# A new order of all steps, with one weight cast cut in two and one PSUM value cut in two, in a explicitly scheduled kernel of gated attention and MLP

## The chip, the cores and the metric

The kernel runs on one core of one Trainium2 chip. The metric is the device time of one execution in microseconds; the kernel before has a median of 178.71 us over three runs (177.62 to 179.46).

## The reference

Two parts follow one another. The first is a recurrence with a gate per element; its result, reshaped to 3072 tokens of 384 values, is the input of an MLP whose activation is h times cos h.

```python
B, H, S, D = 4, 8, 768, 48
f = 1.0 / (1.0 + np.exp(-f_logit))
state = np.zeros((B, H, D, D))
for t in range(S):
    state = f[:, :, t, :, None] * state + np.einsum('bhd,bhe->bhde', k[:, :, t], v[:, :, t])
    y[:, :, t] = np.einsum('bhd,bhde->bhe', q[:, :, t], state)
x = y.transpose(0, 2, 1, 3).reshape(3072, 384)
h = x @ w_in                  # 384 x 2048
out = (h * np.cos(h)) @ w_out # 2048 x 384
```

## The kernel before

**Tiles.** The recurrence is done in chunks of 128 tokens. A *pair* n is two chunks of one batch, 256 tokens with all 8 heads; there are 12 pairs, three to a batch, and the state starts anew with every third. Inside a chunk the gates are summed as logarithms (on TensorE, step `cum`), and q and k are multiplied by the exponentials of that sum and of its negative, so that the chunk becomes ordinary matmuls: scores of k and q, masked, times v, plus q times the state. The MLP takes the 256 tokens of one pair as one *unit* m: eight h steps (step h m.j s: quarter j of the 2048 columns, half s, six matmuls each), four cosines and four products, then for each of its two tiles of 128 tokens four output steps (step o, four matmuls each).

**Engines and steps.** The steps of pair n and unit m, with the lines that they come from:

- loads `f`, `k`, `q`, `v` (L334) and of the weights `w` (L318; `w0.i` is quarter i of w_in, `w1.i` quarter i of w_out), nearly all on SP's queue. Pairs 0 and 1 are loaded by halves (`f0.0`, `f0.1`).
- the weights' casts to bf16, `wc` (L195). A weight quarter is loaded into a buffer that otherwise holds the products g; the buffer is free again when the cast has read it.
- the gate on ACT (ScalarE): `ex`, `ln` (L370, L376), `fx`, `fy` (L387, L390), and after `cum` the exponentials `eb`, `ei` (L470, L474, L479). On POOL (GpSimd) `ad` (L408) sums parts of the logarithms, `ka` and `qa` (L394, L384) multiply by f, `km` and `qm` (L501, L505) make the scaled k and q, called qk.
- q and k transposed: in pairs 0 to 3 by TensorE (`tq`, `tk`, L573) with a copy out of PSUM (`qkt`, L195); in pairs 4 to 11 by DMA transposes from SP's queue (`tq`, L556).
- v spread over the rows that the matmuls want: in pairs 0 and 1 `vb` (L516), then `vs` on TensorE (L529) and two copies `vt`; in the others copies alone.
- TensorE: scores `sc` (L593), state `ps` (L614, L624), outputs `y` and `yi` (L678). DVE (VectorE): the mask `am` (L597), the state's sums and decay `st`, `sz` (L645, L650); `sj` is on TensorE. `xe` (L195) copies y out of PSUM as the MLP's x.
- MLP: `h` (L726) on TensorE, the cosine `co` (L731) on ACT, the product `g` (L708) on DVE, `o` (L747) on TensorE, the copy `ot` (L195) and the store `out` (L758).
- `zf` (L300): matmuls of zeros on TensorE before there is data. `cq`, `z`, `ctl`: constants.

ACT has two tables of functions, one for Exp and Ln and one for Sin; each change of the one for the other is a table load (L790), 12 in the program.

**Order.** `describe` only declares the steps with what they read and write. A string `ORDER` sets the order: one word a step, with its engine (T TensorE, S ScalarE, V VectorE, G GpSimd, Y SyncE) and the numbers of the buffers or PSUM banks that it writes to. `emit` issues the steps in that order; each engine runs its own in that order and waits where an input is missing or a buffer is not yet free. PSUM has eight banks: a value of pool `p1` is one bank, one of `p2` two neighbours, such as every h value (1024 columns) and every score. `apart` tells the framework that steps in different banks of one PSUM tile don't depend on each other. So `co1.2:S1` reads: the second-last cosine of unit 1, on ACT, into buffer 1.

**Course.** PE begins with zeros and the halves of pairs 0 and 1; unit 0's first full h run, step `h0.10`, comes at 24.9 us. Units 0 and 1 are worked together, then 2 and 3, and so on, with the recurrence of later pairs between them. Their h steps come as runs, with cosines and products following: between two such runs ACT does the gates of the next two pairs, with the other table loaded.

## Time and profile before

| | |
|---|---|
| median of three runs | 178.71 us (177.62, 178.71, 179.46) |
| the profiled execution | 179.52 us |
| its span, first to last instruction | 177.7 us |
| TensorE busy, share of the span | 170.9 us, 96% |
| VectorE, ScalarE, GpSimd busy | 74%, 73%, 55% |
| granted TensorE clock over the span | 1.00 |
| DMA | 34.46 MB, mean 194 GB/s |
| last matmul's end to the span's end | 3.0 us |

The device time of the profiled execution is 1.8 us longer than its span. TensorE is the busiest engine by far, but a busy share says little of a single place: between two runs of h steps TensorE works on outputs of the units before, while ACT changes its table, does the gates and changes it back. In a row of a timeline the columns are the start (us), the duration, the engine, the line, the operation with tile names without buffer numbers, and in brackets the idle time before it with what ended it. Rows of a table of windows give the window, its length and then, for PE, PEld (weight loads), DVE, ACT and POOL in this order, the busy time with the number of instructions; last come the granted clock, the share of the DMA engines and GB/s.

### The profile page before, as it was taken

What the parts mean: (1) busy time and instruction counts of PE and PEld (TensorE: products, weight loads), DVE (VectorE), ACT (ScalarE), POOL (GpSimd) and SP (SyncE); (2) the same over time, 40 slices, a digit from 0 to 9 for tenths busy, and PEclk for the clock granted to TensorE, in tenths of its full rate; (3) what the DMA queues carried; (4) which work ended last, traced back from release to release, by engine and by line L of the source; (5) the groups of instructions that cost most, each with busy time, mean ns of one, the idle gap of its engine ahead of it and who ended that gap; (6) DMA issues with size and microseconds to landing.
All of it is one profiled execution on the core that took longest, in us unless ns stands there. A gap on an engine that the chain in (4) does not pass through costs nothing.

```text
span 177.7 us, 5995 instructions
## 1 busy us (share of the span) xinstructions
PE 170.9 (96%) x2565; PEld 126.4 (71%) x2568; DVE 131.9 (74%) x208; ACT 130.0 (73%) x177; POOL 98.3 (55%) x125
## 2 busy tenths in 40 slices
PE   7999999999999999999969999999999999999993
PEld 2576678866778767787647886676786767887762
DVE  6378989786696899799957688878878967274720
ACT  3977698659999999769978789988693644374610
POOL 7042397796579989989737977369993000000000
PEclk9999999999999999999999999999999999999999
DMA  4999999999998999987999999982077040001033
GB/s 128 302 308 355 267 353 315 337 301 311 254 269 204 205 221 227 267 210 133 199 221 284 279 185 268 218 229 76 4 162 162 4 177 4 4 0 44 4 133 133
DMA packets 70330, 34.46 MB, mean 194 GB/s; under 512 B 59296, under 2 KB 68768, under 8 KB 70304
## 3 DMA queue, kind: packets, MB, share of 16 engines
q1 hardware_dynamic: 69744, 33.69, 78.5%
q10 hardware_dynamic: 560, 0.39, 0.8%
q8 instruction: 20, 0.33, 0.8%
q14 instruction: 6, 0.05, 0.2%
HBM read 25.17 MB, written 4.72 MB: 168 GB/s over the span
## 4 chain that ended last, share of the span: by engine, by line
PE 57%; DMA 16%; POOL 10%; SPq 10%; ACT 2%; issue 2%; DVE 1%; POOLq 0%; DVEq 0%
PE ps L747 28%; PE ps L726 21%; SPq L334 8%; DMA k<-in_k_dram 7%; POOL qk L505 6%; DMA q<-in_q_dram 5%; DMA qkt<-qk 4%; PE ps L678 4%; PE ps L593 3%; ACT co L731 1%; SPq L318 1%; POOL q L384 1%; POOL k L394 1%; PE ps L624 1%; POOL vt L195 1%
## 5 line engine op out<-in xcount | busy, mean ns | idle before, releaser
L708 DVE TENSOR_TENSOR g<-ps,co 128x1024 bf16<-128x1024 f32 x48 | 57.9, 1222 | 19.6 <-ACT co L731 18.3
L747 PE MATMUL ps<-w_out_bf,g 128*128 128x384 bf16 (+1 forms) x400 | 68.5, 320 | 0.0
L731 ACT ACTIVATE co<-ps,halfpi 128x1024 bf16<-128x1024 f32 x48 | 52.7, 1113 | 21.1 <-PE ps L726 19.9
L726 PE MATMUL ps<-x,w_in_bf 128*128 128x256 bf16 x576 | 67.4, 273 | 0.0
L726 PEld LDWEIGHTS <-w_in_bf 128*128 128x128 bf16 x576 | 55.4, 98 | 8.5
L747 PEld LDWEIGHTS <-g 128*128 128x128 bf16 x400 | 37.2, 98 | 20.7
L597 DVE TENSOR_TENSOR am<-ps,pmask 128x1024 bf16<-128x1024 f32 x24 | 28.9, 1220 | 6.1 <-PE ps L593 5.8
L790 ACT ACT_TABLE_LOAD x12 | 15.4, 1283 | 1.7 <-PEq L855 1.5
L505 POOL TENSOR_TENSOR qk<-k,bi 128x384 bf16<-128x384 f32 x16 | 16.0, 1000 | 0.5
L505 POOL TENSOR_TENSOR qk<-q,b 128x384 bf16<-128x384 f32 x16 | 15.9, 999 | 0.6
L195 POOL COPY vt<-vb 64x384 bf16<-64x384 bf16 x27 | 13.5, 501 | 1.3
L195 ACT COPY ot<-ps 128x384 f32<-128x384 f32 (+1 forms) x13 | 5.5, 441 | 9.6 <-PE ps L747 9.1
L408 POOL TENSOR_TENSOR sp<-ls 128x384 bf16<-128x384 f32 x8 | 8.0, 998 | 7.9 <-ACT ls L376 7.7
L370 ACT ACTIVATE f<-f 128x768 f32<-128x768 f32 (+1 forms) x14 | 10.2, 746 | 1.3 <-DMA f<-in_f_logit_dram 1.3
L300 PE MATMUL ps<-zero 128*128 128x512 bf16 x31 | 9.6, 434 | 1.6 <-DVE zero L201 1.2
L645 DVE TENSOR_TENSOR ps<-ps,sz 128x192 f32<-128x192 f32 x26 | 9.4, 363 | 1.7 <-PE ps L624 0.9
L593 PE MATMUL ps<-qkt 48*64 48x128 bf16 x384 | 9.1, 220 | 1.5 <-DMA qkt<-qk 1.4
L394 POOL TENSOR_TENSOR k<-k,f 128x384 f32<-128x384 f32 x8 | 8.0, 1002 | 4.4 <-ACT bi L479 2.5
L593 PEld LDWEIGHTS <-qkt 48*64 48x64 bf16 x384 | 6.2, 106 | 5.2 <-issue 2.5
L195 DVE COPY ot<-ps 128x384 f32<-128x384 f32 (+1 forms) x13 | 6.9, 535 | 3.6 <-PE ps L747 3.6
L195 DVE CAST x<-ps 128x384 bf16<-128x384 f32 x14 | 7.3, 552 | 2.7 <-PE ps L678 2.7
L384 POOL TENSOR_TENSOR q<-f,q 128x384 f32<-128x384 f32 x8 | 8.0, 999 | 1.7 <-ACT f L387 1.5
(105 smaller groups left out, 185.9 us busy)
## 6 DMA issues: line engine op xcount, KB each, us to landing
out_dram<-ot SPq DMA_DIRECT2D x22, 192.0 KB, 2.8
f<-in_f_logit_dram SPq DMA_DIRECT2D x10, 384.0 KB, 5.6
k<-in_k_dram SPq DMA_DIRECT2D x10, 384.0 KB, 5.7
q<-in_q_dram SPq DMA_DIRECT2D x10, 384.0 KB, 5.5
v<-in_v_dram SPq DMA_DIRECT2D x10, 384.0 KB, 5.4
g<-in_moe_w_in_dram SPq DMA_DIRECT2D x4, 768.0 KB, 7.2
g<-in_moe_w_out_dram SPq DMA_DIRECT2D x4, 768.0 KB, 8.5
q<-in_q_dram SPq DMA_DIRECT2D x4, 192.0 KB, 4.6
```

What stands on the lines that cost most here:

```text
L195: (nc.scalar.copy if e == "ACT" else eng(e).tensor_copy)(out=o, in_=i)
L334: G.step(name, ("SP", "ACT") if name in ("f0.0", "f0.1") else ("SP",), lambda e: eng(e).dma_start(out=val.ap.rearrange("p (r f) e d -> p r ...
L370: nc.scalar.activation(out=flat(t.ap), in_=flat(t.ap), func=AF.Exp, scale=-1.0)
L384: eng(e).tensor_mul(out=w.ap[:, :, 0, :], in0=t.ap[:, :, 1, :], in1=w.ap[:, :, 0, :])
L505: G.step(f"{nm}{n}.{u}", ("POOL", "DVE") if cut else ("POOL",), lambda e, u=u, j=j, src=src, dec=dec: eng(e).tensor_mul(out=qkp[u][j].ap[: ...
L593: nc.tensor.matmul(o[64 * h:64 * h + 64, r, 2 * a + g, :].rearrange("p (e n) -> p e n", e=2), lhsT=qkv(u)[s, 1, a, g, h, :], rhs=qkv(u)[s, ...
L597: G.step(f"am{n}.{u}", ("DVE",), lambda e, u=u, sc=sc: nc.vector.tensor_mul(out=am[u].ap.rearrange("p r b n -> p (r b) n"), in0=sc.ap.rear ...
L708: nc.vector.tensor_mul(out=o.rearrange("p b (n e) -> p b n e", e=2), in0=ph.ap.rearrange("p (b e n) -> p b n e", e=2, n=64), in1=co.ap.rea ...
L726: nc.tensor.matmul(ph.ap[:, i * T:(i + 1) * T].rearrange("p (g t) -> p g t", t=C), lhsT=w_in_bf[:, kk, f0:f0 + 128], rhs=xa[:, :, kk, :], ...
L731: G.step(f"co{m}.{j}", ("ACT",), lambda e, ph=ph, co=co: nc.scalar.activation(out=co.ap, in_=ph.ap, func=AF.Sin, bias=halfpi), reads=[ph], ...
L747: nc.tensor.matmul(po.ap[:, 0:w], lhsT=gT.ap[:, j, i * C:(i + 1) * C], rhs=w_out_bf[:, j, a * w:a * w + w], start=(po.first and j == 4 * s ...
L790: nc.scalar.preload_act_table_set(TABLES[s.table])
```

## The change

Four things change in the code; the other lines are as before (those behind the insertions stand 2 to 10 lines lower, so L556 becomes L565 and L790 becomes L800).

1. `ORDER` is replaced as a whole: order, engines, buffers and banks. Steps on SP 103 to 102 (`f0.1` goes to ACT's queue), on ACT 169 to 177, on VectorE 188 to 186, on GpSimd 113 to 109. GpSimd gives up `km0.1`, `km3.0` and `km3.1` (to VectorE) and `wc1.3` (to ACT). The two-tile value of the last tile but one, tile 22, was cut in two already and stays so.
2. `ZEROS` goes from 34 to 30.
3. The cast `wc0.0` of the first quarter of w_in is two steps, one for each half of the columns: `wc0.00`, now on ACT, and `wc0.01`, on GpSimd. An h step that needs one half waits for that alone.
4. In pairs 0 and 1 the spread v is two values of one PSUM bank each instead of one of two banks. One step `vs` still writes both; each copy `vt` reads one.

```diff
-ZEROS = 34
+CUT_W = ((0, 0),)
+ZEROS = 30
...
 ORDER = """
...
-w1.3:Y4 tk2.1:T3 tq2.1:T h1.31:T4 h1.30:T co0.2:S0 tq2.0:T2 g0.2:V tk2.0:T co1.3:S2 wc1.0:G h1.21:T6
...
-qm7.1:G tq7.1:Y1 q8:Y2 h5.11:T vt6.0:G o7.2:T0 qa6:G co5.1:S1 qm6.1:G tq6.1:Y3 o7.3:T vt6.3:S g4.1:V
...
+wc0.3:G h0.20:T0 g1.1:V0 co1.0:S1 h0.21:T qm2.1:G tk2.1:T3 g1.0:V co0.2:S2 h1.31:T4 f4:Y2 qm2.0:G
...
+co4.1:S1 tq7.1:Y3 h5.21:T qm6.1:G st6.10:V vb7:S0 o6.0:T g4.1:V tq6.1:Y1 vt6.0:G0 co5.2:S3 h5.11:T2
...
         G.step(f"w{part}.{i}", ("SP",), fetch, writes=[stage])
-        G.step(f"wc{part}.{i}", ("POOL", "ACT"), lambda e: copy(e, dst.ap, view()),
-               reads=[stage], writes=[dst])
+        if (part, i) not in CUT_W:
+            G.step(f"wc{part}.{i}", ("POOL", "ACT"), lambda e: copy(e, dst.ap, view()),
+                   reads=[stage], writes=[dst])
+            return
+        for a in range(2):
+            cols = lambda t, a=a: t[:, :, a * w // 2:(a + 1) * w // 2]
+            to = dst.part(cols)
+            G.step(f"wc{part}.{i}{a}", ("POOL", "ACT"), lambda e, to=to, cols=cols: copy(e, to.ap, cols(view())),
+                   reads=[stage], writes=[to])
...
-            pv = Val(p2)
+            pv = [Val(p1), Val(p1)]
...
-                                rows = pv.ap.rearrange("p (g x) -> p g x", g=2)[64 * x:64 * x + 64, g, 0:DM]
+                                rows = pv[g].ap[64 * x:64 * x + 64, 0:DM]
...
-                    pv.ap[:, 512 * g:512 * g + DM].rearrange("p (h d) -> p h d", d=D)), reads=[pv], writes=[vtp[g]])
+                    pv[g].ap[:, 0:DM].rearrange("p (h d) -> p h d", d=D)), reads=[pv[g]], writes=[vtp[g]])
...
-                G.step(f"h{m}.{j}{s}", ("PE",), first, reads=[xw, w_in_v[(j * F + s * F // 2) // 4]],
+                wv = w_in_v[(j * F + s * F // 2) // 4]
+                G.step(f"h{m}.{j}{s}", ("PE",), first, reads=[xw, wv.parts[s] if wv.parts and F == 4 else wv],
```

In `ORDER` the new string differs everywhere. Three places bear on the prediction.

**ScalarE from the table load behind unit 1's cosines to the gate of pair 5.** Names: `ps_...` is a PSUM tile, `g_...` the staging buffer of a weight. Before, `f_101` is the gate of pair 4 and `f_99` that of pair 5, `qkt_139` the copy `qkt3.0`, the cast is `wc1.2`:

```order
L195 COPY qkt_139<-ps_170 128x1024
L790 ACT_TABLE_LOAD
L370 ACTIVATE f_101<-f_101 128x768
L376 ACTIVATE ls_115<-f_101 128x768
L390 ACTIVATE f_101<-ls_115 128x8x48
L195 COPY vt_136<-vb_128 64x8x48
L387 ACTIVATE f_101<-f_101 128x8x48
L195 CAST w_out_bf<-g_156 128x1536
L195 COPY vt_136<-vb_128 64x8x48 x2
L195 COPY vt_134<-vb_126 64x8x48
L195 COPY ot_164<-ps_171 128x384
L370 ACTIVATE f_99<-f_99 128x768
```

The same stretch after; here `qkt_137` is `qkt3.0`, `g_158` holds `w1.3` and `g_156` `w1.2`:

```order
L800 ACT_TABLE_LOAD
L379 ACTIVATE f_101<-f_101 128x768
L197 COPY qkt_137<-ps_172 128x1024
L385 ACTIVATE ls_115<-f_101 128x768
L197 CAST w_out_bf<-g_158 128x1536
L396 ACTIVATE f_101<-f_101 128x8x48
L197 COPY vt_136<-vb_128 64x8x48 x2
L197 CAST w_out_bf<-g_156 128x1536
L399 ACTIVATE f_101<-ls_115 128x8x48
L197 COPY vt_136<-vb_128 64x8x48
L197 COPY ot_166<-ps_171 128x384
L197 COPY vt_134<-vb_127 64x8x48
```

The table load now stands ahead of `qkt3.0`, which has moved behind the first Exp of pair 4, and a second cast, `wc1.3`, stands in the stretch; behind the Exp and Ln of pair 5 follows an x copy, `xe2.0`, that VectorE did before.

**SyncE at the load of pair 4's gate.** `f_101` is `f4`, `g_158` is `w1.3`, `k_105` (before) and `k_104` (after) are `k3`. Before:

```order
L334 DMA k_105<-in_k_dram 128x8x96
L318 DMA g_158<-in_moe_w_out_dram 128x4x384
L334 DMA f_101<-in_f_logit_dram 128x8x96
L334 DMA v_109<-in_v_dram 128x8x96
L318 DMA g_156<-in_moe_w_out_dram 128x4x384
```

After, the same five loads:

```order
L343 DMA k_104<-in_k_dram 128x8x96
L343 DMA f_101<-in_f_logit_dram 128x8x96
L320 DMA g_158<-in_moe_w_out_dram 128x4x384
L343 DMA v_109<-in_v_dram 128x8x96
L320 DMA g_156<-in_moe_w_out_dram 128x4x384
```

The load of `f4` and that of `w1.3` have changed places.

**SyncE at the transposes of pairs 7 and 6.** `qk_125` is the scaled q and k of pair 7, `qk_124` that of pair 6; `q_108` is `q8` before. Before:

```order
L334 DMA f_99<-in_f_logit_dram 128x8x96
L334 DMA f_101<-in_f_logit_dram 128x8x96
L556 DMA_TRANSPOSE qkt_139<-qk_125 128x8x128
L556 DMA_TRANSPOSE qkt_138<-qk_125 128x8x128
L334 DMA q_108<-in_q_dram 128x8x96
L556 DMA_TRANSPOSE qkt_140<-qk_124 128x8x128
L758 DMA out_dram<-ot_166 128x384
L758 DMA out_dram<-ot_163 128x384
L556 DMA_TRANSPOSE qkt_137<-qk_124 128x8x128
L334 DMA q_107<-in_q_dram 128x8x96
```

And after:

```order
L343 DMA f_101<-in_f_logit_dram 128x8x96
L343 DMA f_102<-in_f_logit_dram 128x8x96
L565 DMA_TRANSPOSE qkt_139<-qk_125 128x8x128
L565 DMA_TRANSPOSE qkt_140<-qk_125 128x8x128
L565 DMA_TRANSPOSE qkt_138<-qk_124 128x8x128
L565 DMA_TRANSPOSE qkt_137<-qk_124 128x8x128
L768 DMA out_dram<-ot_164 128x384
L343 DMA q_107<-in_q_dram 128x8x96
```

The load of `q8` no longer stands between the transposes, and the two stores that stood ahead of the last of them are gone from there.

Two smaller places that the prediction uses: at the start, SyncE's last load of the halves is `v1.1` where it was `k1.1`; and behind `vs1`, TensorE's order has `sj1.0` before the state of pair 1. The score steps of pair 3, `sc3.0` and `sc3.1`, stood side by side and now have output steps and `sc3.1` ahead of `sc3.0` between them.

## The prediction

> **What bounds the kernel now.** I read the page's busy shares first, then a table of windows, then the chain of waits, then the timelines of the engines at the few places where TensorE (PE) stands still.

> ```profile
> PE 170.9 (96%) x2565; PEld 126.4 (71%) x2568; DVE 131.9 (74%) x208; ACT 130.0 (73%) x177; POOL 98.3 (55%) x125
> 24.90:174.70 149.80, 148.06 (x2151) 111.43 (x2144) 113.83 (x157) 111.59 (x145) 87.77 (x103) 1.00 0.79 181
> ```

> The second row is a window: its length, then each engine's busy time. From 24.9 us, where the first full tile of the MLP begins (step h0.10), until the last matmul, PE is idle for 149.80 - 148.06 = 1.74 us, at full clock (1.00). From h0.10 on both orders hold the same 270 PE steps. So behind that point the change can only win what PE waits, lose new waits, or move the point itself; behind the last matmul the same copies and stores follow in both, 3.0 us to the span's end at 177.7.

> The waits, from PE's own timeline and the chain:

> ```profile
> 30.84 0.40 PE L573 MATMUL ps<-ident,qk 128*128 128x128 bf16 x4 [0.24 <-POOL qk L501]
> 85.23 4.07 PE L747 MATMUL ps<-w_out_bf,g 128*128 128x384 bf16 x24
> 90.75 0.64 PE L593 MATMUL ps<-qkt 48*64 48x128 bf16 x32 [1.45 <-DMA qkt<-qk]
> 82.75 1.02 POOL qk L505 x2
> 83.77 6.95 DMA qkt<-qk
> 79.37 3.15 SPq L556 DMA_TRANSPOSE qkt<-qk  x2
> 82.58 0.57 SPq L334 DMA_DIRECT2D q<-in_q_dram  x1
> 83.77 1.24 SPq L556 DMA_TRANSPOSE qkt<-qk  x1
> DMA to landing us min/median/max: 3.0/3.5/6.9
> ```

> One wait is large. At 90.75 the scores sc6.1 begin 1.45 us late: their transposed operand (tq6.1) left SP at 83.77, when POOL's last product for it was done, and took 6.95 us, the longest of 16 (median 3.5, last row). A load of q (q8, 82.58) stood ahead of it.

> The second thing to see is a stretch where PE never waits and yet is paced by others:

> ```profile
> 39.27 1.01 ACT L195 COPY qkt<-ps 128x1024 bf16<-128x1024 bf16 x1 [1.93 <-PE ps L573]
> 40.30 1.28 ACT L790 ACT_TABLE_LOAD   x1
> 41.59 0.84 ACT L370 ACTIVATE f<-f 128x768 f32<-128x768 f32 x1
> 44.60 1.46 ACT L195 CAST w_out_bf<-g 128x1536 bf16<-128x1536 f32 x1
> 47.92 0.84 ACT L370 ACTIVATE f<-f 128x768 f32<-128x768 f32 x1
> 50.57 0.49 ACT L479 ACTIVATE bi<-ps 128x384 f32<-128x384 f32 x1
> 52.41 1.28 ACT L790 ACT_TABLE_LOAD   x1
> 53.71 4.18 ACT L731 ACTIVATE co<-ps,halfpi 128x1024 bf16<-128x1024 f32 x4
> 54.85 4.62 DVE L708 TENSOR_TENSOR g<-ps,co 128x1024 bf16<-128x1024 f32 x4 [1.40 <-ACT co L731]
> 41.60:53.70 12.10, 12.10 (x238) 8.56 (x237) 9.90 (x20) 11.84 (x19) 8.49 (x11) 1.00 1.14 276
> ```

> From 41.59 to 53.7 ACT (ScalarE) is busy 11.84 of 12.10 us, without a pause worth naming; the cosines can start only at 53.71, behind the second table load. The products g follow on DVE, 4.62 us for four, so the second ends near 54.85 + 2 x 1.16 = 57.2. Four PSUM pairs of banks hold the first products h of this run; a later one takes the pair that the second g frees (h2.01 here), so it can't begin before 57.2, and PE, without an idle moment there, arrives just then. ACT's second table load sets that moment as much as PE does.

> **The change part by part.** The sum is made against the profiled execution (179.52 us, span 177.7), which lies 0.81 above the median of the runs, 178.71; I carry the difference over to the median.

> The start. Before h0.10, PE waits for loads. The one that lands last ahead of the weights:

> ```profile
> 12.02 5.83 DMA k<-in_k_dram
> 17.39 0.94 ACT L516 ACTIVATE vq<-v,odd 128x768 bf16<-128x768 f32 x1
> 19.70 0.52 PE L529 MATMUL ps<-vq,qsel 64*64 64x192 bf16 x16
> 21.82 0.82 PE L726 MATMUL ps<-x,w_in_bf 128*128 128x256 bf16 x6
> L195 POOL CAST w_in_bf<-g 128x1536 bf16<-128x1536 f32 x4 | 5.9, 1465 | 5.5 <-DMA g<-in_moe_w_in_dram 5.5
> L300 PE MATMUL ps<-zero 128*128 128x512 bf16 x31 | 9.6, 434 | 1.6 <-DVE zero L201 1.2 <-issue 0.3
> ```

> It is k1.1, at 17.85; now v1.1 is last, behind the same bytes, so at about 17.85 too. Then vb1.0 on ACT (0.94) gives 18.85, and PE has vs1 and everything up to h0.10 before it. In this trace PE needs 24.90 - 19.70 = 5.2 us from vs1 to h0.10; sj1.0, which now stands behind vs1, adds 0.26 and a wait of sc1.1 for DVE's copy perhaps 0.2: 18.85 + 5.2 + 0.45 = 24.5, a gain of 0.4, between 0.9 (neither counts) and a loss of 1.0 (v1.1 landing 1.4 later). The halved cast of w_in costs POOL 0.73 instead of 1.465 and ACT about 0.8 (half of its 1.46 for a whole w_out cast, 0.73, is the low end); PE reaches h0.00 after both, so it is hidden by PE's own work; uncovered it would cost the 0.8. The two single-bank values for spread v cost nothing: same matmuls, same copies. Four zero matmuls fewer are 4 x 0.215 = 0.9 us of filler before data (9.6 us for 31, the first ones slow); PE would otherwise wait there, so I count nothing, and 0.9 if they were in the way.

> None of this is a term yet, because the ACT stretch takes it back. With the wait at 30.84 gone too (the q-transpose now comes three h steps later), PE would stand 1.0 us ahead at 57. What ACT allows is less. Its new order moves the table load ahead of qkt3.0, whose 1.93 us of waiting it fills: behind the cosine of h0.31 the load starts at about 36.2 instead of 40.30. Then three more pieces of work stand in the stretch: the qkt3.0 copy (1.01), a second w_out cast, wc1.3 (1.46), and an x copy, xe2.0 (0.48). The first Exp needs f4, which SP now issues right behind k3, ahead of w1.3:

> ```profile
> 29.45 0.50 SPq L334 DMA_DIRECT2D k<-in_k_dram  x1
> DMA to landing us min/median/max: 7.4/7.4/7.4
> 20.00:40.00 20.00, 19.71 (x312) 15.88 (x302) 17.25 (x21) 13.84 (x14) 16.59 (x14) 1.00 1.09 316
> ```

> k3 landed at 36.9. The DMA engines were full (share 1.09) at 316 GB/s, at which the 384 KB of f4 take 1.25 us and the 768 KB of w1.3 2.5. So I put f4's landing at 38.4, and at 40.4 or more where it stood before. From there, each step as long from start to start as the trace has its kind (large activations 0.88, small ones 0.43): 38.4 + 0.88 (ex4) + 1.01 + 0.87 (ln4) + 1.46 + 0.43 + 0.92 (two vt) = 43.97, then wc1.2 1.48, fx4 and vt2.1 0.93, ot3 and vt3.2 0.85 = 47.23. The Exp of f5 can't start before f5 lands:

> ```profile
> 39.53 1.32 SPq L334 DMA_DIRECT2D f<-in_f_logit_dram  x1
> DMA to landing us min/median/max: 7.8/7.8/7.8
> ```

> That is 39.53 + 7.8 = 47.35; before it started at 47.92. From it to the table load are 52.41 - 47.92 = 4.49 us, plus 0.43 for xe2.0, less 0.15 for a short wait on PE: the load at 47.35 + 4.77 = 52.12 and the cosines 0.3 earlier than now. So the term is **-0.3**; ACT reaches f5 with 0.1 us to spare. The low end is -1.0 (f5 lands 0.7 earlier, PE's whole lead kept), the high end +1.6 (f4 lands 2 us later, as before the swap).

> The transposes. POOL's work from ad5 to the last product for tq6.1 is one 0.5 us copy less, and ad5 starts with ln5's end, about 0.6 earlier. Here it ran 49.79 to 83.75, of which 1.3 were waits:

> ```profile
> 49.79 0.99 POOL L408 TENSOR_TENSOR sp<-ls 128x384 bf16<-128x384 f32 x1 [1.86 <-ACT ls L376]
> 65.40 1.00 POOL L408 TENSOR_TENSOR sp<-ls 128x384 bf16<-128x384 f32 x1 [0.50 <-ACT ls L376]
> 76.32 1.00 POOL L394 TENSOR_TENSOR k<-k,f 128x384 f32<-128x384 f32 x1 [0.67 <-ACT co L731]
> ```

> So the product is ready at 49.2 + 33.96 - 0.5 = 82.6, or 81.3 without those waits, and q8 no longer stands between the transposes. With 3.1 us to land (the two at 79.37 were 2 us apart, so they don't hold each other up) that is 85.7; with 6.95 it is 89.6. sc6.1 now comes at about 88.5 in PE's order. I take **-1.45** (nearer to the median landing of 3.5); the far end leaves 1.1 of the wait.

> PE's tilings. The order splits sc3.0 from sc3.1, so behind h0.10 stand 22 stretches of small-tile matmuls instead of 21. What a stretch costs beside full-size steps:

> ```profile
> 94.60 0.76 PE ps L747 x4
> 95.36 0.65 PE ps L726 x6
> 159.69 0.65 PE ps L747 x4
> ```

> An output step of four matmuls takes 0.65 among its like and 0.76 next to such a stretch, 0.11 at each edge: **+0.2** for one stretch, 0 to 0.5. [...]

> Sum: -0.3 - 1.45 + 0.2 = -1.55, so 177.97 for the execution profiled and 178.71 - 1.55 = **177.2** for the median. One per cent, 1.79 us here, is about what a measurement of this kernel can tell from no change.

> **The rivals.**
> A, the larger gain: f5 lands earlier and ACT doesn't hold PE back. For it: from 18 to 47 us SP waited for staging buffers of the weights (row below), which are now handed out in another order, so loads may be issued sooner. Against it: the DMA engines were full (1.09 and 1.14 in the window rows), so fewer waits of SP bring no bytes. Then -1.0 - 1.45 = -2.45, 176.3.

> ```profile
> SPq L318 <- POOL w_in_bf L195: 5.1, 2, 3.6
> ```

> B, the wait was this execution's own. For it: the fastest run is 177.62, 1.9 under the profiled one, and a transpose of 6.95 stands alone. Against it: the median is nearer to the profiled one. Then a typical run gains only the 0.3, less 0.2 for the stretch, 178.6.

> C, slower: ACT's stretch becomes the new bound. Its place is between the two table loads. For it: 2.9 us of work more and only 0.1 to spare before f5, and the first Exp now waits for f4 with qkt3.0 and wc1.3 behind it. Against it: the table is there four us earlier. Each us that f4 lands after 38.5 delays the cosines, and PE with them, by one: with f4 1.65 us later than I put it, the gain is gone. Behind the 2.5 us of bytes of w1.3 and the 1.25 of one load more it lands 3.75 later, 3.65 past what ACT has to spare: -0.3 + 3.65 - 1.45 + 0.2 = +2.1, 180.8.

> **How the numbers follow.** Forecast 0.42, A 0.26, B 0.14, C 0.18. The forecast's own range is 176.2 to 178.0, and 0.16 of its 0.42 lies under 176.9; with A that is 0.42 for faster by over 1%. Of C I put 0.10 over 180.5. The rest, 0.48, is within 1%. Range 175.8 to 179.3: A with the run-to-run spread at the low end, half of C at the high end.

> **What would show it.** Right: no wait of sc6.1 and sc7.1 over 0.3 us near 88; two table loads near 36 and 52, ACT filled between; the first cosine behind the second at 53.4; span near 176.2. Wrong: first cosine after 55 (C); h0.10 after 25.5, or waits of PE over 0.5 us at places that I don't name (before sc9.0, or where cum6 waits for POOL); a first cosine before 52.9 (A).

## The result, and the profile after

The change makes the kernel slower. Its median is 180.47 us (179.71 to 181.75, six runs) against 178.63 us for the kernel before (six runs): the ratio is 1.0122, with a 95% interval of 1.0085 to 1.0158. That is 1.84 us more, where 1.5 us less was forecast, and above the range.

The profiled execution of the change took 179.71 us, the shortest of its six, and that of the kernel before 179.52 us, above its six others. So these two traces lie closer together (spans 177.9 and 177.7) than the medians. Later I took five more traces of the change and one more of the kernel before (`before_again`, span 176.7, an execution of 178.52 us), and the reading below is over all of them.

The busy shares have hardly moved, except that ScalarE does more and GpSimd less:

```profile
PE 171.3 (96%) x2562; PEld 126.1 (71%) x2564; DVE 131.2 (74%) x206; ACT 135.4 (76%) x184; POOL 92.4 (52%) x121
```

The table of windows, from the first full h run (h0.10) to the end of the last matmul, first of the change, then of the second execution of the kernel before:

```profile
25.08:174.88 149.80, 148.79 (x2152) 111.14 (x2144) 113.06 (x157) 115.12 (x149) 83.45 (x100) 1.00 0.77 178
```

```profile
25.44:173.70 148.26, 148.01 (x2151) 111.33 (x2144) 114.46 (x157) 111.58 (x145) 87.72 (x103) 1.00 0.78 181
```

The same TensorE steps take 1.5 us longer, at full clock. In the first trace of the kernel before, 1.45 us of this stretch was one wait at sc6.1; in the second there is no such wait. What the change waits for instead stands in TensorE's own timeline:

```profile
76.04 1.16 PE L735 MATMUL ps<-x,w_in_bf 128*128 128x256 bf16 x9 [0.20 <-issue]
92.06 0.34 PE L431 MATMUL ps<-sp,incl 128*128 128x384 bf16 x1 [0.44 <-DVE am L606]
95.05 0.39 PE L735 MATMUL ps<-x,w_in_bf 128*128 128x256 bf16 x2 [0.27 <-DVE x L197]
```

```profile
143.25 0.42 PE L602 MATMUL ps<-qkt 48*64 48x128 bf16 x16 [0.44 <-DMA qkt<-qk]
```

The first three rows are from the change's first trace, the last from its fourth (`after_d`). They are four places: a pause inside the step h4.21, so that h4.20 comes late, without a releaser ("issue"), a wait of cum8 and one of h7.21 for VectorE, and a wait of sc10.1 for a DMA transpose. A bracket shows less than a step loses (0.20 in the first row, where h4.20 comes 0.39 late). So I measure each place as the time from step to step above the usual time of such a pair of steps in the first trace of the kernel before. In us:

| execution | span | h0.10 | tq2.1 | h4.20 | sc6.1 | cum8 + h7.21 | h5.30 | sc10.1 | all the rest |
|---|---|---|---|---|---|---|---|---|---|
| before | 177.7 | 24.90 | 0.40 | 0 | 1.52 | 0 | 0 | 0 | 0.45 |
| before_again | 176.7 | 25.44 | 0 | 0 | 0 | 0 | 0.37 | 0 | 0.44 |
| before_code | 177.4 | 25.07 | 1.07 | 0 | 0.41 | 0 | 0 | 0 | 0.41 |
| after | 177.9 | 25.08 | 0 | 0.39 | 0 | 1.05 | 0 | 0.28 | 0.84 |
| after_again | 177.8 | 25.12 | 0 | 0.62 | 0 | 0.77 | 0 | 0.17 | 0.85 |
| after_c | 178.1 | 25.56 | 0 | 0.47 | 0 | 0.91 | 0 | 0 | 0.90 |
| after_d | 178.8 | 25.67 | 0 | 0.37 | 0 | 0.96 | 0 | 0.63 | 0.87 |
| after_e | 177.7 | 24.94 | 0 | 0.56 | 0 | 1.04 | 0 | 0 | 0.89 |
| after_f | 178.3 | 25.33 | 0 | 0.63 | 0 | 0.97 | 0 | 0.24 | 0.86 |

`before_code` is the order of before in the changed code (below). The pause at h4.20 and the waits of cum8 and h7.21 are there in all six executions of the change, that of sc10.1 in four; their means are 0.51, 0.95 and 0.22, together 1.68 us. The large waits of the kernel before come and go.

### The profile page after: what moved, and what is told of

Same layout as the page of the kernel before. It is cut to its first block, busy times and chain, and to the rows that moved or that the text cites. A ratio compares the mean times of both kernels' runs of the same rounds, so it can differ in the third digit from the quotient of the medians.

```text
span 177.9 us, 5989 instructions
## 1 busy us (share of the span) xinstructions
PE 171.3 (96%) x2562; PEld 126.1 (71%) x2564; DVE 131.2 (74%) x206; ACT 135.4 (76%) x184; POOL 92.4 (52%) x121
## 4 chain that ended last, share of the span: by engine, by line
PE 61%; POOL 10%; DMA 10%; ACT 8%; DVE 5%; SPq 2%; issue 2%; POOLq 0%; DVEq 0%; ACTq 0%
PE ps L735 25%; PE ps L757 24%; POOL qk L514 5%; PE ps L687 3%; DMA f<-in_f_logit_dram 3%; DMA k<-in_k_dram 3%; PE ps L602 3%; DMA out_dram<-ot 2%; DMA qkt<-qk 2%; POOL vt L197 2%; ACT co L741 2%; POOL q L393 2%; DVE g L717 1%; ACT f L379 1%; DVE am L606 1%
## 5 line engine op out<-in xcount | busy, mean ns | idle before, releaser
L741 ACT ACTIVATE co<-ps,halfpi 128x1024 bf16<-128x1024 f32 x48 | 52.9, 1114 | 15.6 <-PE ps L735 13.5
L197 ACT COPY ot<-ps 128x384 f32<-128x384 f32 (+1 forms) x14 | 6.5, 466 | 14.9 <-PE ps L757 14.9
L197 DVE COPY ot<-ps 128x384 f32<-128x384 f32 (+1 forms) x12 | 6.0, 503 | 9.3 <-PE ps L757 7.8
L302 PE MATMUL ps<-zero 128*128 128x512 bf16 x28 | 9.0, 435 | 1.3 <-DVE zero L203 1.2
L197 POOL CAST w_in_bf<-g 128x1536 bf16<-128x1536 f32 (+1 forms) x4 | 5.4, 1340 | 7.3 <-DMA g<-in_moe_w_in_dram 7.3
```

The costliest lines, as they stand in the source:

```text
L197: (nc.scalar.copy if e == "ACT" else eng(e).tensor_copy)(out=o, in_=i)
L302: G.step(f"zf{i}", ("PE",), lambda e, dump=dump: nc.tensor.matmul(dump.ap, lhsT=zero[:, 0:128], rhs=zero, start=True, stop=True), writes=[ ...
L741: G.step(f"co{m}.{j}", ("ACT",), lambda e, ph=ph, co=co: nc.scalar.activation(out=co.ap, in_=ph.ap, func=AF.Sin, bias=halfpi), reads=[ph], ...
```

## The experiments

Orders are shown as words of the order string. Each ratio is against the kernel before on the same chip. A copy of the kernel before itself came out at 0.9955 (0.9923 to 0.9987), so differences of half a per cent between ratios are carried here by the traces, not by the times alone.

**Which half of the program loses: two splices.** Up to the step y5 (73 us) one order, behind it the other, with buffers and banks renamed to fit.

```diff
 before_then_y5:  -order of before behind y5   +order of the change behind y5
 after_then_y5:   -order of the change behind y5   +order of before behind y5
```

> The order of before up to the step y5 (73 us), the order of the change behind it (slots of buffers and banks renamed so that what is live fits; nothing else). Theories 1 and 3: the loss is in the second part: ratio to before 1.009 to 1.013. Theory 2: 0.999 to 1.003.

> The order of the change up to the step y5 (73 us), the order of before behind it. Theories 1 and 3: the loss is not in the first part: ratio to before 0.998 to 1.003. Theory 2: 1.009 to 1.013.

Measured: 1.0150 (1.0108 to 1.0192) and 1.0060 (1.0025 to 1.0095). Neither ratio lies in a range that I had given. The second part of the new order loses for certain; for the first part, 0.6 per cent is little more than the 0.45 by which the copy of the kernel before differs. The trace of the first splice shows 1.07 at cum8 and h7.21 and 0.30 at sc10.1, as the change does, and 0.58 at sc6.1, which no execution of the change has. That of the second shows the pause of 0.84 at h4.21 from the new order and 0.48 at sc6.1 from the old one.

**The copy that waits for a store.** In the change's trace VectorE stands still ahead of the copy ot7 at 90.31:

```profile
88.17 0.62 DVE L659 TENSOR_TENSOR sz<-ps,b 128x192 bf16<-128x192 f32 x2
90.31 0.56 DVE L197 COPY ot<-ps 128x384 f32<-128x384 f32 x1 [1.52 <-DMA out_dram<-ot]
90.78 2.35 DVE L606 TENSOR_TENSOR am<-ps,pmask 128x1024 bf16<-128x1024 f32 x2
94.44 0.55 DVE L197 CAST x<-ps 128x384 bf16<-128x384 f32 x1
```

Output buffer 1, which ot7 is to write, still holds the tile of ot2. Its store out2 stands behind four transposes on SyncE. The first row is out2 in the kernel before, ahead of all four; the second has the last three transposes in the change, the third its out2:

```profile
71.86 2.70 SPq L758 DMA_DIRECT2D out_dram<-ot  x1
82.08 4.01 SPq L565 DMA_TRANSPOSE qkt<-qk  x3
86.14 0.57 SPq L768 DMA_DIRECT2D out_dram<-ot  x1
```

```profile
L768 SPq DMA_DIRECT2D out_dram<-ot x1: 574/574/574, 86.1 to 86.1; - x1
  DVE ot L197: 1.5, 1
DMA to landing us min/median/max: 4.1/4.1/4.1
```

In the change it left at 86.14 and landed 4.1 us later. Behind ot7 on VectorE stand the masks am7.1 and am6.1 (90.78) and then the x copies (94.44). cum8 writes to bank 5, which am7.1 reads, and h7.21 needs the x copies. That is 1 us on TensorE. The test gives ot7 another buffer:

```diff
-ot7:V1  ot9:S3  ot11:V1  ...
+ot7:V3  ot9:S1  ot11:V3  ...
```

> The changed kernel once more, for a second trace. All theories: ratio to before 1.012 (180.5). Theory 1 (the copy ot7 on VectorE waits for the store out2, which stands behind DMA transposes on SyncE; the mask am7.1, cum8 and the x copies behind it come late, 1.05 us of PE waits at 92 and 95 in the first trace): the wait of ot7 and the waits at cum8 and h7.21 are at least as large, 1.0 to 2.0 together, where the run is longer. Theory 2 (the loss lies before 73 us: a later h0.10, a later first cosine of the second h run): h0.10 after 25.3 or co2.1 after 54.2. Theory 3 (the loss lies behind 110: sc10.1 waits for tq10.1, which stands behind the store out15): a wait at sc10.1 over 0.5, where the first trace has 0.28.

> From ot7 on the output buffers 1 and 3 change names, so that ot7 writes to the buffer that out4 left at 77.6 and not to that of out2; nothing else moves. Theory 1: VectorE's wait of 1.5 us ahead of ot7 goes, the waits at cum8 and h7.21 fall under 0.3 together, and the time falls by 0.75 to 1.8: 178.7 to 179.7, ratio to before 1.001 to 1.006. Theories 2 and 3: no change, 1.012.

On the same chip the unchanged change has 1.0104 (1.0068 to 1.0139, 179.90 us) and this 1.0046 (1.0023 to 1.0068, 178.96 us). The trace of `after_again` has 0.77 at cum8 and h7.21 together, less than the 1.0 to 2.0 that I had expected of a longer execution; it was no longer than the first. In `after_ot7` buffer 3 is free in time (its store out4 landed at 77.6), VectorE goes straight on, and the waits at cum8 and h7.21 are gone:

```profile
88.47 0.62 DVE L659 TENSOR_TENSOR sz<-ps,b 128x192 bf16<-128x192 f32 x2
89.01 0.55 DVE L197 COPY ot<-ps 128x384 f32<-128x384 f32 x1
89.69 2.36 DVE L606 TENSOR_TENSOR am<-ps,pmask 128x1024 bf16<-128x1024 f32 x2
```

So one buffer number costs 0.94 us, about half of the loss. Theory 1 of the expectations stands for that half.

**Did the 1.45 us at sc6.1 matter in the kernel before?**

```diff
 before_again: (nothing)
 before_q8:
-qm7.1:G tq7.1:Y1 q8:Y2 h5.11:T ...   tq6.0:Y0 o9.3:T
+qm7.1:G tq7.1:Y1 h5.11:T ...   tq6.0:Y0 q8:Y2 o9.3:T
```

> The kernel before, for a second trace. Theory of the prediction: sc6.1 waits 1.0 to 1.6 us for tq6.1 again. Theory B: it waits less than 0.5, and the last matmul ends about 1 us earlier than in the first trace, near 173.5.

> The kernel before with one word of its order moved: the load q8 stands behind the four transposes of pairs 7 and 6 on SyncE instead of between them. Theory of the prediction (the 1.45 us wait at sc6.1 is what a typical run pays, and q8 is in its way): faster by 1.1 to 1.5, ratio to before 0.992 to 0.994. Theory B (that wait was the one execution's own): ratio 0.998 to 1.002, and no wait over 0.5 at sc6.1 in its trace.

In `before_again` the load q8 stands at the same place and tq6.1 lands 4.9 us after its issue at 84.0, at 88.9, and sc6.1 doesn't wait:

```profile
L556 SPq DMA_TRANSPOSE qkt<-qk x1: 1281/1281/1281, 84.0 to 84.0; - x1
DMA to landing us min/median/max: 4.9/4.9/4.9
```

So the wait was largely the first execution's own, as rival B had it. Without q8 between them (`before_q8`) three of the four transposes land in 3.06 us, which is what the prediction said of the mechanism, and sc6.1 has no wait; but the time is 181.22 us, ratio 1.0109 (1.0054 to 1.0164): slower, as neither expectation had it. The one execution traced is the longest of the six, 183.04 us. In it a copy again waits for a store: ot8 stands behind out9, whose buffer it takes:

```profile
98.88 0.56 DVE L195 COPY ot<-ps 128x384 f32<-128x384 f32 x1 [3.62 <-DMA out_dram<-ot]
```

```profile
99.50 3.70 PE L726 MATMUL ps<-x,w_in_bf 128*128 128x256 bf16 x20 [2.73 <-DVE ot L195]
```

Three of the other five took 180.13 to 180.35 us; whether they have this wait, no trace shows. To test it, ot8 got the buffer of ot4, and out4 was issued early enough:

```diff
 before_q8_ot8, against before_q8:
-... out6:Y ...   f11:Y3 ... out4:Y   ot8:V0
+... out6:Y out4:Y ...   f11:Y3 ...   ot8:V2
```

> before_q8 with two more words changed: the store out4 stands behind out6 on SyncE (it stood behind f11), and from ot8 on the output buffers 0 and 2 change names, so that ot8 writes to the buffer that out4 leaves at about 91 and not to that of out9. Theory buffer (in before_q8 the copy ot8 waited for out9, issued 92.2 and landed 98.8, behind the later loads; TensorE stood 2.7 us for its bank before h5.30 and ran at half pace for 1.2 us more): the wait at h5.30 falls under 0.5, no wait at sc6.1, ratio to before 0.994 to 0.999. Rival (the late q8 itself costs: qa8 on GpSimd waits for it and what follows comes late): the wait at h5.30 stays over 1 us, ratio 1.006 or more.

The wait at h5.30 is gone, and sc6.1 has none; but the ratio is 1.0118 (1.0069 to 1.0166). In the trace (179.45 us, its shortest execution) TensorE waits later, for GpSimd and for a transpose of its products:

```profile
114.38 0.32 PE L422 MATMUL ps<-sp,incl 128*128 128x384 bf16 x1 [0.40 <-POOL sp L408]
115.85 0.42 PE L593 MATMUL ps<-qkt 48*64 48x128 bf16 x16 [0.37 <-DMA qkt<-qk]
```

GpSimd's qa8 began at 93.61 and ka9 at 96.55, where `before_again` has 92.62 and 95.17. So neither expectation holds whole: the buffer made the wait at h5.30, but without it the kernel is as slow. That the late q8 makes the new waits is not shown: the sum ad10, which cum10 waits for here, had itself waited 1.94 us for ScalarE. How the 1.2% divides is open.

**The pause without a releaser.** At h4.20 nothing in the profile holds TensorE. The trace's DMA records have 20 transfers of 16 KB in the queue of kind "instruction", which the page sums as (q8 is the queue's number here, not the load)

```profile
q8 instruction: 20, 0.33, 0.8%
```

TensorE runs 2564 weight loads and as many matmuls, 5128 instructions, which is 20.03 times 256; so I took one transfer for 256 of them, an estimate from these two counts. Below, instructions are numbered in this order, load, matmul, load. One transfer lies just ahead of the pause:

```
                16 KB transfer    instruction 2495 starts
before          72.54 to 73.75    75.24   no pause
before_again    72.78 to 74.02    75.38   no pause
after           73.47 to 74.70    76.03   0.39
after_again     73.55 to 74.80    76.31   0.62
after_ot7       73.49 to 74.68    76.33   0.64
after_then_y5   73.79 to 75.01    76.56   0.84
after_z15       73.90 to 75.14    77.49   no pause
```

In the four rows with a pause the transfer starts 0.9 to 1.3 us later than in the first trace of before, and TensorE goes on 1.3 to 1.7 us after it ends, at its 2495th instruction each time. In the kernel before this instruction also comes 1.4 to 1.5 us after the transfer, without a pause: there the code may come just in time, which is not shown. Two experiments aimed at this (the last row is one of them):

```diff
 after_fix3, against after_ot7:
-q7:Y2 k8:Y2 ...   f9:Y3   ...  out15:Y tq10.1:Y3
+q7:Y2 ...   f9:Y3 k8:Y2   ...  tq11.0:Y2 tq10.1:Y3 ...  out15:Y
 after_z15, against after_ot7:
-ZEROS = 30
+ZEROS = 15   (every second word zf left out)
```

> The change with three words moved or renamed: the output buffers 1 and 3 change names from ot7 on (as in after_ot7); the load k8 stands behind f9 on SyncE instead of ahead of out4; the transpose tq10.1 stands behind tq11.0 instead of behind the store out15. Theory code (the pause of 0.4 to 0.8 us of TensorE inside the steps h4.21 and h4.20, at its 2495th instruction, is a wait for instructions, whose 16 KB transfer at 73.5 stands behind data loads): with 384 KB less ahead of it the transfer starts up to 1.2 us earlier, before 73.0, and the pause falls under 0.3. Theory steps (the pause belongs to these steps, by their banks or operands): it stays at 0.4 to 0.8. Queue theory for tq10.1: it leaves SyncE at about 133.5 instead of 138.25 and the wait at sc10.1 goes. Time with all three: 0.5 to 1.0 below after_ot7, ratio to before 0.999 to 1.002; without the code part 1.002 to 1.004.

> after_ot7 with every second of the 30 zero matmuls at the start left out (15 matmuls with their weight loads, 30 instructions of TensorE fewer; nothing of the computation). Theory code (the pause in h4.21 and h4.20 is a wait for the next 16 KB of instructions, 256 of them): the limit falls 30 instructions later in the program, at h4.31 or h4.30, where TensorE arrives over 1 us later, so the pause is gone or under 0.2; the time falls by 0.4 to 0.7 against after_ot7 (ratio to before 1.000 to 1.002) if the start is no later. Theory steps (the pause belongs to h4.20 itself): it stays there at 0.4 to 0.8, ratio 1.0046.

Moving k8 did not do what I said: the transfer started at 73.78, 3.1 us after TensorE's 2239th instruction as in `after_ot7`, and the pause of 0.30 is only a little under the 0.37 to 0.85 of other executions. So what holds the transfer back is not that load; it stays open. Leaving out 30 instructions at the start, which by that estimate moves the limit of a block 30 instructions down the program, did what I said: the transfer starts no earlier, but the 2495th instruction now belongs to h4.30 and comes 2.35 us after it. The pause is gone, without any touch on these steps, as 27 matmuls in one row show where the change has a break:

```profile
75.61 3.13 PE L735 MATMUL ps<-x,w_in_bf 128*128 128x256 bf16 x27
```

Times: 0.9984 (0.9959 to 1.0010) for `after_fix3` and 0.9984 (0.9953 to 1.0015) for `after_z15`. The span of `after_z15` is 0.67 us below that of `after_ot7`, which is the pause of 0.64; the ratios, taken on two chips, lie further apart. More pauses of the kind came up in other executions, at TensorE's instructions 448 (first row below, `after_fix3_z15`) and 704 (second fence, `after_f4`, whose second row is 2495 again):

```profile
19.56 0.22 PE L687 MATMUL ps<-am,vt 128*32 128x128 bf16 x1 [0.72 <-issue]
```

```profile
23.58 0.70 PE L735 MATMUL ps<-x,w_in_bf 128*128 128x256 bf16 x5 [0.50 <-issue]
77.37 1.38 PE L735 MATMUL ps<-x,w_in_bf 128*128 128x256 bf16 x11 [0.67 <-issue]
```

448 and 704 are 256 apart, and 704 and 2495 seven times 256 less 1. (The expectations below say 449 and 705.) The pause at 2495 goes with the instruction's number and not with the step, from which I take it for a wait for code; the profile names no releaser. With 30 zero matmuls nine traces have it in h4.21, 0.30 to 0.85 us; `after_then_y5`, where h4.20 comes first, has it in h4.20. With 34 zeros ahead of the same new order (`before_then_y5`, `start_before`) pauses of 0.2 and 0.4 us stand at instructions 2493 and 2492, which then belong to ps6.0, and h4.21 has none. With 15 zeros three traces have none. That the pauses at 448 and 704 are of the same kind is argued from their distance alone.

**The transpose behind a store.** In the change tq10.1 stands behind out15 on SyncE, which waits for o15's copy:

```profile
130.75 2.62 SPq L565 DMA_TRANSPOSE qkt<-qk  x2
137.82 0.34 SPq L768 DMA_DIRECT2D out_dram<-ot  x1
138.25 1.24 SPq L565 DMA_TRANSPOSE qkt<-qk  x1
```

Its last product was ready at 132.65; in the kernel before tq10.1 left at 130.68. In `after_fix3` it leaves with tq11.0 (131.5 to 132.9) and sc10.1 has no wait. Alone on top of `after_z15`:

```diff
-out15:Y tq10.1:Y3
+tq11.0:Y2 tq10.1:Y3 ...  out15:Y
```

> after_z15 with the transpose tq10.1 behind tq11.0 instead of behind out15 (k8 left where the change has it). Queue theory: no wait at sc10.1, where six traces of the change have 0 to 0.63 (mean 0.22); 0.2 below after_z15: ratio to before 0.996 to 0.999. Rival (what is saved at sc10.1 is waited for behind it): 0.9984, as after_z15.

1.0002 (0.9970 to 1.0034): no wait at sc10.1, but `after_z15` had none in its trace either, and 0.2 us can't be seen in the time.

**Does ScalarE pace the second h run?**

```diff
 after_f4, against after_ot7:
-f4:Y2 ... w1.3:Y4
+w1.3:Y4 f4:Y2
```

> after_ot7 with the loads f4 and w1.3 in the order of before (w1.3 first). Theory ACT (ScalarE's work between the two table loads sets when the second cosines start, and TensorE's pace with it): f4 lands 1.3 to 3 us later than 37.4, ex4 starts as much later less 0.9, the first cosine co2.1 1 to 2 us later than 53.65, and the time rises by as much: ratio to before 1.009 to 1.017. Rival (TensorE sets the pace there, ScalarE has room): co2.1 later, but h3.31 still near 59.9 and the ratio 1.003 to 1.006.

f4 landed at 39.66, 2.2 us later than in `after_ot7`, and the Exp of pair 4 waited for it. The ratio is 1.0062 (1.0038 to 1.0087), which speaks for the rival:

```profile
39.68 0.85 ACT L379 ACTIVATE f<-f 128x768 f32<-128x768 f32 x1 [0.52 <-DMA f<-in_f_logit_dram]
47.77 0.48 ACT L197 COPY ot<-ps 128x384 f32<-128x384 f32 x1 [0.25 <-PE ps L757]
53.18 1.28 ACT L800 ACT_TABLE_LOAD   x1
54.47 2.21 ACT L741 ACTIVATE co<-ps,halfpi 128x1024 bf16<-128x1024 f32 x2
```

h0.10 came at 25.96 here (behind the pause of 0.50 at instruction 704). From there to the first cosine are 54.47 - 25.96 = 28.51 us. In the change's first trace it is 53.60 - 25.08 = 28.52, and in the other five 28.51 or 28.52. In the kernel before it is 53.71 - 24.90 = 28.81, 28.41 without the wait of 0.40 at tq2.1, and 28.38 in `before_again`, which has no such wait. Where TensorE loses time in this stretch, the cosine moves by as much: by 1.07 us in `before_code` (29.43) and by 0.50 in `after_fix3_z15` (29.02). Counted from h0.10, which was itself 0.83 us later, the Exp of pair 4 was only 0.51 us later than in `after_ot7`, where it starts 0.9 us behind f4's landing; ScalarE had made that up by the Exp of pair 5. So TensorE sets the pace, and ScalarE has room for at least 0.5 us; a larger delay was not tried.

**The edits of the code alone.**

```diff
 before_code: the changed code with CUT_W and the two single-bank values,
-ZEROS = 30, order of the change
+ZEROS = 34, order of before (wc0.0:G as wc0.00:G wc0.01:G)
```

> The order of before in the code of the change: spread v as two values of one bank, the cast of the first quarter of w_in as two steps, both on GpSimd, 34 zero matmuls. The prediction's terms (nothing from either): ratio to before 0.998 to 1.002, h0.10 at 24.9 to 25.5. Rival (the two halves one behind the other delay h0.01 and all that follows): h0.10 at 25.7 or later, as in the trace of before_then_y5, ratio 1.002 to 1.005.

1.0007 (0.9976 to 1.0037), h0.10 at 25.07: they cost and bring nothing that can be measured.

**Two misses.** A splice of before's first 25 us with `after_ot7` was to price the start, and `after_fix3` with half the zeros was to be the best version.

```diff
 start_before:    -order of the change up to h0.11   +order of before up to h0.11
 after_fix3_z15:  -ZEROS = 30   +ZEROS = 15
```

> The order of before up to the step h0.11 (25 us) with the cast of the first quarter of w_in whole and 34 zero matmuls, the order of after_ot7 behind it. Theory start (the first 25 us of the change cost 0.2): h0.10 at 24.9, ratio to before 1.003 to 1.005. Theory no start (nothing lost there): 1.0046 as after_ot7, h0.10 at 25.1 or later.

> after_fix3 with 15 zero matmuls instead of 30, as the best version that the runs point to. Theory code: the pause of 0.30 that is left in h4.20 goes; 0.3 below after_fix3, ratio to before 0.995 to 0.998. Theory steps: 0.998 as after_fix3.

The first came out at 1.0202 (1.0150 to 1.0254) for a reason of its own: the splice put g0.0 into the buffer that w0.3 is cast from, TensorE waited 2.4 us for it at 31.65, and its time says nothing of the start; h0.10 came at 25.14. The second has 1.0017 (0.9982 to 1.0052). Its trace has no pause at h4.20, as forecast, but one at instruction 448, h0.10 at 26.39 and a wait of 0.50 at h1.10 for the x copy. No version here beats the kernel before.

**More executions of the unchanged change** (no edit), to see where typical ones lose:

> The change, unchanged, for one more trace. Both traces so far are shorter (177.9, 177.8) than most executions (median near 178.6 of span), so 0.7 us of the loss has no place yet. Theory code: a longer execution has further pauses of TensorE without a releaser at its instructions 449 or 705 (256 apart, and 7 times 256 below 2495), each 0.5 to 1.0, or a longer one at 2495. Theory store: ot7 waits longer for out2, and cum8 and h7.21 lose more than 1.1 together. Theory start: h0.10 after 25.6 by waits that have a releaser.

> As after_c: one more execution of the change; the three theories and their numbers are the same.

> As after_c: one more execution of the change; the three theories and their numbers are the same.

> As after_c: one more execution of the change; the three theories and their numbers are the same.

They took 179.89, 180.54, 179.47 and 180.10 us; their rows are in the table above. None shows a new large place, and in none do cum8 and h7.21 lose more than 1.1. `after_d`, the longest, has a pause of 0.4 at instruction 704, 0.63 at sc10.1 and h0.10 at 25.67. So the spread from 177.7 to 178.8 is made of the start, the pauses without a releaser and that transpose. The longest execution of the change, 181.75 us, has no trace.

## Why the prediction was wrong, point by point

**The start (h0.10 at 24.5 forecast).** It came at 24.94 to 25.67, mean 25.28, which is no earlier than before (24.90 and 25.44). The last load landed earlier than I put it in five of six traces (v1.1 at 16.30 to 18.08, 17.85 forecast), but vs1 does not wait for it. VectorE is late with its half of v, and TensorE has two zero matmuls ahead of vs1:

```profile
18.10 0.55 DVE L499 TENSOR_TENSOR qk<-q,bq 128x384 bf16<-128x384 f32 x1
18.84 0.61 DVE L527 TENSOR_SCALAR vq<-v,odd 128x768 bf16<-128x768 f32 x1
19.30 0.59 PE L302 MATMUL ps<-zero 128*128 128x512 bf16 x2
19.82 0.52 PE L538 MATMUL ps<-vq,qsel 64*64 64x192 bf16 x16
```

VectorE's half of v for pair 1 (vb1.1) ends at 19.45, behind the products of pair 1, and two of the zeros, which I had taken for mere filler, hold vs1 until 19.82; I had 18.85 from ScalarE's half alone.

**ScalarE's stretch (-0.3).** The times came out near the forecast (the Exp at 38.4, the second table load at 52.12, the cosines at 53.4), but in part by luck. I had the Exp wait for f4 at 38.4; f4 landed at 37.10, and the Exp waited for the table load, which began at 37.00 and not at 36.2.

```profile
37.00 1.28 ACT L800 ACT_TABLE_LOAD   x1
38.30 0.84 ACT L379 ACTIVATE f<-f 128x768 f32<-128x768 f32 x1
39.44 1.01 ACT L197 COPY qkt<-ps 128x1024 bf16<-128x1024 bf16 x1 [0.30 <-PE ps L582]
46.89 0.48 ACT L197 COPY ot<-ps 128x384 f32<-128x384 f32 x1 [0.34 <-PE ps L757]
47.80 0.84 ACT L379 ACTIVATE f<-f 128x768 f32<-128x768 f32 x1
52.30 1.28 ACT L800 ACT_TABLE_LOAD   x1
53.60 1.11 ACT L741 ACTIVATE co<-ps,halfpi 128x1024 bf16<-128x1024 f32 x1
```

What failed is the sentence that "what ACT allows is less": the distance from h0.10 to the first cosine goes by TensorE (above), and a ScalarE without a pause was one that just kept up. Nor did f5 bind, which landed at 45.78 and not at 47.35. The term is 0 by this stretch. The wait at tq2.1, whose end I had let ScalarE take back, is a gain of 0 to 1.07 by the three traces.

**The transposes (-1.45).** The mechanism was right and its price was not. With q8 away the four land like this, and sc6.1 and sc7.1 wait for none:

```profile
L565 SPq DMA_TRANSPOSE qkt<-qk x4: 1237/1283/2658, 78.9 to 84.8; - x4
DMA to landing us min/median/max: 3.1/3.3/5.7
```

The transpose tq6.1 took 6.95, 4.88 and 5.97 us in three traces with q8 ahead and 3.23 to 3.40 in the six of the change. (In `before_then_y5`, also without q8 ahead, it took 4.81.) But I priced the wait by one execution, and that was an unusual one: it was 1.52, 0 and 0.41 in three traces of before's order. Rival B named this and I gave it 0.14; its own time of 178.6 missed too, since it has no room for the new waits.

**The tilings (+0.2).** All small excesses together are 0.41 to 0.45 in before's order and 0.84 to 0.90 in the change, +0.43, about twice the term. That the difference is all of this kind is not shown.

**What I left out** is the loss: 0.95 for the store that holds VectorE, 0.51 for the pause at instruction 2495, 0.22 for tq10.1 behind a store. The step of the prediction that failed is the sum -0.3 - 1.45 + 0.2: it has no term for new waits of TensorE behind h0.10, which the runs show as +1.68. The sentence ahead of it, "the change can only win what PE waits, lose new waits, or move the point itself", was true, but I looked for new waits at ScalarE's stretch alone (rival C) and didn't walk the new order of the output buffers against that of the stores on SyncE, where out2 had moved behind the transposes. That is in the orders and needed no run. The pause at instruction 2495 is not: nothing in the old trace shows it. My sign of being wrong, waits over 0.5 us at places that I don't name, came true at cum8 (0.61 in the first trace).

The second step that failed is the size of -1.45, a wait that three traces of the old order have at 0 to 1.52. So how much the change loses depends on the execution of the old order that it is held against. Against `before_again`, whose 178.52 us lies nearest to the median, the waits are 2.54 us on average with the rest, against 0.81; with a start 0.16 earlier this makes 1.6 us, where the spans differ by 1.4 (178.1 on average, against 176.7) and the medians by 1.6 to 1.8. Against the mean of the three traces of the old order (177.3) the spans differ by 0.8 only. How often the old order has its waits at tq2.1 and sc6.1, three traces can't say.

## What to carry to other kernels

When an order is changed, follow each buffer in a small ring to the instruction that frees it and to the queue which that stands in: a store behind four transposes held a copy, the copy held VectorE's queue, and TensorE paid 0.95 us for it two engines away. A wait in one trace is a sample; before it is priced as a gain, a second execution of the unchanged kernel says whether it is there. An engine that is busy without a pause is not yet the bound: the distance between two fixed events over several executions (28.51 us here, also with ScalarE's first Exp 0.5 us late) tells who paces whom.

## What the runs showed of the hardware that I had not expected

**Pauses of 2.7 and 2.4 us were followed by granted clocks of 0.55 over 3.1 us and of 0.50 over 3.4 us.** The last but one column is the DMA share, the one ahead of it the granted clock; the first fence is `before_q8` (waiting from 96.7 on), the second `start_before` (from 29.2 on):

```profile
96.70:99.50 2.80, 0.07 (x2) 0.01 (x1) 0.62 (x2) 1.51 (x2) 2.42 (x3) 0.89 1.11 259
99.50:102.60 3.10, 3.10 (x17) 2.25 (x18) 2.00 (x3) 0.00 (x0) 3.10 (x4) 0.55 0.90 224
```

```profile
31.60:35.00 3.40, 3.35 (x18) 2.49 (x18) 2.36 (x3) 1.67 (x3) 1.98 (x3) 0.50 1.11 323
```

In the second row 17 matmuls of h take 3.10 us, where at full clock six take 0.65 (the row at 95.36 of the first trace of the kernel before): so the wait of 2.7 us cost about 1.3 us more behind it (an estimate from these rows). The wait of 1.45 us at sc6.1 left the clock of the kernel before at 1.00 (90 to 95 us).
